# Another written-out order of the pieces, the last output columns in two writes, and w2 in one load

## The chip, the core and the metric

The kernel runs on one NeuronCore of a Trainium2 chip. The metric is the time of one execution on the device in microseconds (us). All engines of the core run side by side, each in its own order: TensorE (PE in the profile, its weight loads PEld), VectorE (DVE), ScalarE (ACT), GpSimd (POOL) and SyncE (SP). SyncE, ScalarE and GpSimd also issue DMAs, which run on 16 DMA engines.

## The reference

A block of 2048 tokens of width 640 (bf16). The input is normalized, and the normalized input feeds two branches whose outputs are added to the input.

```python
def reference(A_x, A_wqkv, A_wo, B_x, B_w1, B_b1, B_w2, B_b2):
    x = A_x                                  # (1, 2048, 640)
    xn = _layernorm(x, axis=-1)
    return x + _A_ref(xn, A_wqkv, A_wo) + _B_ref(xn, B_w1, B_b1, B_w2, B_b2)

# A: 32 heads of 20; each token looks at 8 tokens: itself and those 2, 4, ... 14 before it
qkv    = x @ wqkv
logits = einsum("bhsd,bhswd->bhsw", q, k[gathered]) * 20 ** -0.5   # masked before the start
o      = einsum("bhsw,bhswd->bhsd", softmax(logits), v[gathered])
A      = o @ wo                                                    # 640 x 640
# B: dense, 640 -> 1536 -> 640
B      = gelu_tanh(x @ w1 + b1) @ w2 + b2
```

## The kernel before

The tokens are cut into four chunks of 512 (n = 0 to 3), each into four blocks of 128 (bl). The work is cut into some 700 named pieces. `make_plan` lists them with what they need, and `ORDER` writes out by hand the order in which they are issued. As each engine runs its instructions in the order in which they are issued, `ORDER` sets the order on every engine and every DMA queue at once; when a piece starts is then left to semaphores. A name begins with its kind, and its digits are the chunk and a part:

| pieces | engine | what they do |
|---|---|---|
| `st`, `rs`, `rc`, `xn` | DVE, ACT, DVE, ACT | layernorm: statistics, standard deviation, its reciprocal, normalized x (for chunk 0 DVE normalizes) |
| `tc` | SP | the normalized block transposed by DMA (for chunk 0 `tp` on PE and a copy `tc`) |
| `ga` `gb` `gd` `ge` `gc`, `hj` and `hc` | PE and ACT | projections q, k, v of chunk 0 in parts, and the copies out of PSUM; `hj2..` reads the weights wv |
| `pj`, `pc` | PE, ACT | projections of chunks 1 to 3 (digits: chunk, q/k/v, columns), and the copies out of PSUM |
| `qk`, `lg` | DVE, PE | products q * shifted k for two window places of a pair each; sum over a head's 20 columns into the logits (80 matmuls per chunk) |
| `m` `mx` `ex` `ss` `ri` `at` | DVE (`ex` on ACT) | softmax over the 8 places |
| `xd`, `xs` | SP, ACT | the attention weights written out to all 128 partitions by DMA (tile `ax`), two quarters by each queue |
| `av`, `ad`, `ot` | DVE | products v * weights (8 per chunk), their sums, and oT |
| `f1`, `ge` | PE, ACT | first matmul of the dense branch (12 per chunk) and GELU; hT has 18 buffers |
| `o`, `oc`, `od` | PE, ACT, POOL | output of one block in five parts (four over hT and w2, the fifth over oT and wo), the copy out of PSUM, and the DMA that adds it to the output in DRAM; two buffers osb |
| `xp`, `xb` | SP or ACT, POOL | x copied into the output, and b2 added to it there, by DMA |
| `ld` | SP | the loads of w2, wo and b2 |
| `ohi`, `oclo`, `ochi` | PE, DVE | the last block: its last 128 columns on PE, and the additions of x with the writes to DRAM |

All accumulators of `pj`, `f1`, `hj` and of some `o` share four buffers in PSUM (`acc`). The products of `qk` and `av` share four buffers (`prod`); `prod` of a window pair is free again when its `lg` has read it. For the last block there is no accumulating DMA: `oclo` adds x to the first 512 columns and issues their write from SyncE, then PE does `ohi`, then `ochi` adds x to the last 128 columns and issues their write from ScalarE.

The functions that the change touches, and what calls them, with the lines of the profile:

Of the kernel before, what the change touches and what calls it, by code (L numbers as in the profile page):

```python
# [62 lines left out]
S, D, F, H, W, DIL = 2048, 640, 1536, 32, 8, 2  # L63
P = 128
DH = D // H
PAD = (W - 1) * DIL
KT, FT = D // P, F // P
CH = 512
# [8 lines left out]
LASTB = S // P - 1  # L77
# [5 lines left out]

ORDER = """
pad01 pad02 st00a st00 sm rs00 me nm rc00 sq xn00a xn00b tp00a tp00b tc00a rs01 tb ga tc00b rc01 xn01 gb2 b1 tp01
gb3 tc01a tc01b gb4 gd gc0 ge st03a hj101 gc4 st03 st02a rs03 hj102 st02 hc101 hj100 rs02 hc102 rc02 rc03 gc1 hj200
xn03 xn02 hc100 st11a tp03 tp02 st13a tc03 hj201 st11 tc02 st10a hj202 hc200 st12a hj012 st10 hj010 st13 hc012 hc202
st12 hj111 hc010 hc201 hj011 rs1 hc111 rc1 st21a hj110 hc011 st22a st22 hj112 hc110 st20a hj212 st33a hc112 f102
xn10 qk031 hc212 f100 xn13 tc10 qk001 ge02 f109 qk020 hj210 pad11 tc13 ge09 hj211 qk010 xn11 f108 hc211 qk000 ge00
f101 tc11 qk011 f105 ge01 ge08 qk021 f104 xn12 f1011 tc12 ge04 qk030 f1010 ge011 st23a st21 lg00 ge010 st20 ld lg01  # L90
ge05 st23 lg02 lg03 st31a rs2 pj114 mk m0 pj102 pc114 st32a st30a pj110 pc102 mx0 hc210 pj111 pc110 st32 ex0 pj101
rc2 st31 st30 pj100 st33 pj112 ss0 pc100 pc101 pj104 xn21 ri0 pj103 tc21 pc104 at0 pc111 pj113 pc103 pc112 pj123
pc113 xn23 qk120 f113 pc123 tc23 xn22 f103 qk111 pj121 ge03 qk121 f118 xd0 qk130 ge13 f107 ge18 f112 qk100 ge07
pad21 f106 ge12 qk110 xs0 f115 ge06 qk131 xw0 f110 rs3 qk101 o020 tc22 xn20 o021 ge15 lg10 lg11 av011 lg12 pc121
tc20 lg13 ge10 rc3 pj120 av000 o022 pc120 av031 xn32 o023 pj122 tc32 av021 f111 pc122 m1 xn30 pj124 ge11 av030 tc30
pad12 pj214 av020 pj204 pc214 pj203 pc204 av001 pj211 pc203 av010 pc124 pj202 xn33 mx1 pc211 pj210 tc33 xn31 ad01
pj221 pc210 pc202 pj223 tc31 pj201 ad00 pj220 pc201 pc223 pj213 xp0 pj200 pc213 ad02 pc221 pj212 pc220 pc200 pj224
pc212 ex1 xb0 ot0 pj310 f1110 qk231 pc310 o024 qk220 pj300 oc02 ss1 pad31 od02 o000 o001 qk200 o002 o003 ri1 o004
at1 pj313 qk201 xd1 oc00 o010 pc313 qk211 pc300 pj301 xs1 qk210 o011 o012 qk221 o013 xw1 pj303 qk230 o014 xp1 xb1
lg20 oc01 lg21 av130 pc303 lg22 pc224 lg23 av100 o030 f138 av110 o031 od00 ge38 av111 pj312 o032 pc301 m2 ge110 f117  # L100
pc312 av131 f116 av120 pj304 pj302 mx2 o033 pc302 av121 ge16 f121 ge17 ad11 f1111 xp2 f1210 ge21 xb2 ge111 o034
ge210 av101 pad22 pc304 f119 ad10 pj311 pj222 pc311 xb3 oc03 pj314 ad12 ge19 od01 f114 od03 f125 ge14 pc222 ot1
pj324 pad32 pc314 ex2 o100 qk331 pj322 qk321 o101 ge25 o102 ss2 o103 pj323 ri2 o104 qk330 pc323 pc322 pj320 at2 oc10
pj321 pc320 qk311 xd2 xs2 o110 pc324 qk301 o111 pc321 o112 qk310 f120 qk300 f126 xw2 f130 ge26 qk320 f127 xl lg30
ge27 lg31 av201 lg32 lg33 o113 m3 o114 av211 f1311 oc11 av200 od11 o120 o121 od10 av221 o122 av230 o123 o124 av220
f1211 oc12 mx3 od12 o130 av210 o131 ge20 ge30 f124 ex3 ad20 f123 o132 ge311 o133 av231 o134 ge24 ss3 f128 ge211 oc13
f129 ad21 ge23 f122 ge29 ge28 f131 ge22 ri3 o210 at3 f135 ad22 o211 xd3 f134 f1310 ot2 o212 ge310 ge31 o213 xs3 o214
xw3 f137 oc21 ge34 od21 o220 av311 o221 o222 av300 o223 av310 o224 f136 av321 oc22 od22 o230 av301 o231 od13 o232
av320 o233 av331 o234 av330 f132 oc23 od23 o200 ad31 o201 ge32 ge36 o202 ge37 f139 ad30 f133 ge39 ge35 o203 ge33
o204 ad32 o310 oc20 o311 o300 ot3 o301 o302 o303 o304 o312 oc30 o313 od30 o320 od20 o321 o322 o323 o314 o324 oc31  # L110
od31 o330 oc32 o331 od32 o332 o333 o334 ohi oclo ochi
""".split()


# [173 lines left out]
def kernel(  # L288
# [16 lines left out]
    nc = tc.nc  # L305
# [3 lines left out]
    out_sd = out.rearrange("b s d -> (b s) d")  # L309
# [22 lines left out]
    w2_sb = wts.tile([P, FT, D], BF16, name="w2_sb")  # L332
# [27 lines left out]


    def do_ld():
        w2_v = B_w2.rearrange("(t p) n -> p t n", p=P)
        for c in range(2):
            ts = slice(c * FT // 2, (c + 1) * FT // 2)
            nc.sync.dma_start(w2_sb[:, ts, :], w2_v[:, ts, :])
        nc.sync.dma_start(wo2[:], A_wo.rearrange("(p t) n -> p t n", t=KT))
        nc.sync.dma_start(b2bc[:], b2_bcast)

# [392 lines left out]
    def do_ochi():  # L762
        osb = tiles["osb", last]
        nc.vector.tensor_tensor(  # L764
            out=osb[:, CH:D], in0=tiles["hi", *last][:, 0 : D - CH], in1=x_sb[:, LASTB, CH:D], op=ALU.add
        )
        nc.scalar.dma_start(out_sd[LASTB * P :, CH:D], osb[:, CH:D])

    fns = {k[3:]: v for k, v in locals().items() if k.startswith("do_")}
    engines = {getattr(mybir.EngineType, e) for e in ("PE", "DVE", "Activation", "SP")}  # L770
# [40 lines left out]
```

## Time and profile before

| | |
|---|---|
| median of 13 runs | 212.66 us (212.34 to 216.91) |
| the profiled execution | 212.47 us |
| its span, first to last instruction | 210.5 us |
| granted TensorE clock | 1.00 in every stage |
| busy: PE, DVE, ACT, POOL | 205.5, 173.4, 111.6, 19.8 us |
| matmuls recorded, weight loads recorded | 1511, 1535 |
| bytes moved by DMA | 23.93 MB, 114 GB/s in the mean |

A matmul is recorded with the time until its result is out of the array, 379 ns for 512 columns, while the next one starts 216 ns after it; busy times of an engine are unions, so overlap is not counted twice. "Idle before" is the time for which an engine had stood still when an instruction began, with what ended it; a row with SPq or ACTq is the issue of a DMA, and not the transfer. Some matmul records are missing from a trace.

### The profile page before, as it was taken

To read this page: it belongs to the slowest core of one execution; us is meant where nothing else is said; L and a number is where in the kernel's file an instruction comes from. 1 tells how busy PE (TensorE), PEld (TensorE's weight loads), DVE (VectorE), ACT (ScalarE), POOL (GpSimd) and SP (SyncE) were. 2 spreads that over 40 slices of the span, in tenths; PEclk is the share of its full clock that TensorE was granted. 3 is DMA by queue.
4 is the path that set the end of the run, shared out by engine and by line. 5 is a ranking of instruction groups with operands and counts; after the bars stand their busy time and mean duration, and the time that the engine had idled before them with its cause. 6 is when DMAs were issued, how large, how long until landed. Compare 5 with 4: busy or idle time off the path is not lost.

```text
span 210.5 us, 3645 instructions
## 1 busy us (share of the span) xinstructions
PE 205.5 (98%) x1511; PEld 118.8 (56%) x1535; DVE 173.4 (82%) x178; ACT 111.6 (53%) x193; POOL 19.8 (9%) x37
## 2 busy tenths in 40 slices
PE   8999999999999999999999999999999999999994
PEld 2999656554465555555654555565554455555552
DVE  3487999969979999996899999989999829997001
ACT  6476977889785748330727486321396221441120
POOL 2000000000000002110300600101101011101130
PEclk9999999999999999999999999999999999999999
DMA  6999417914952063559296690721222571212224
GB/s 218 367 364 372 85 36 200 384 42 86 142 68 46 16 189 45 85 91 217 78 156 219 97 152 3 139 93 11 27 28 34 100 125 17 29 27 31 31 27 70
DMA packets 24072, 23.93 MB, mean 114 GB/s; under 512 B 9080, under 2 KB 21880, under 8 KB 24056
## 3 DMA queue, kind: packets, MB, share of 16 engines
q1 hardware_dynamic: 17008, 14.68, 25.6%
q0 software_dynamic: 4144, 4.92, 17.3%
q10 hardware_dynamic: 2904, 4.10, 7.1%
q8 instruction: 12, 0.20, 0.4%
q14 instruction: 4, 0.03, 0.0%
HBM read 10.00 MB, written 7.54 MB: 83 GB/s over the span
## 4 chain that ended last, share of the span: by engine, by line
PE 96%; DMA 1%; issue 1%; ACT 1%; DVE 0%; ACTq 0%
PE lo L734 27%; PE hps L703 24%; PE pps L509 23%; PE hi L736 8%; PE gps L553 6%; PE L L608 4%; PE gps L522 1%; DMA x_sb<-in_A_x_dram 1%; PE tp L465 1%; ACT xn L417 0%; DVE xn L450 0%; ACT std L430 0%; DVE osb L764 0%; DVE rstd L434 0%; ACT L376 0%
## 5 line engine op out<-in xcount | busy, mean ns | idle before, releaser
L703 PE MATMUL hps<-xnT,w_sb 128*128 128x512 bf16 x235 | 55.1, 379 | 0.3
L681 DVE TENSOR_TENSOR pv<-vT,ax 128x2560 bf16<-128x2560 bf16 x32 | 45.8, 1483 | 9.1 <-DMA ax<-attn 7.1
L734 PE MATMUL lo<-w_sb,hT 128*128 128x512 bf16 x184 | 52.9, 379 | 0.1
L583 DVE TENSOR_TENSOR prod<-qT,kT 128x2560 bf16<-128x2560 bf16 x32 | 45.5, 1484 | 1.9 <-ACT kT L568 1.5
L714 ACT ACTIVATE hT<-hps,b1T 128x512 bf16<-128x512 f32 x48 | 31.6, 689 | 18.7 <-PE hps L703 17.2
L736 PE MATMUL hi<-w_sb,hT 128*128 128x128 bf16 x192 | 40.3, 219 | 0.5 <-issue 0.2
L703 PEld LDWEIGHTS <-w_sb 128*128 128x128 bf16 x240 | 22.8, 98 | 26.0
L690 DVE TENSOR_TENSOR pv<-pv 128x5120 bf16<-128x5120 bf16 x12 | 33.7, 2821 | 0.2
L741 ACT CAST osb<-lo 128x512 bf16<-128x512 f32 x15 | 8.8, 586 | 44.7 <-issue 26.7
L734 PEld LDWEIGHTS <-hT 128*128 128x128 bf16 x192 | 18.7, 98 | 22.5 <-issue 0.4
L734 PE MATMUL lo<-wo,oT 128*128 128x512 bf16 x74 | 21.9, 379 | 0.0
L747 POOL DMA_DIRECT2D out_dram<-osb x15 | 13.6, 904 | 86.3 <-ACT osb L742 80.3
L736 PEld LDWEIGHTS <-hT 128*128 128x128 bf16 x192 | 18.4, 98 | 2.7
L509 PE MATMUL pps<-xnT,wk_sb 128*128 128x512 bf16 x73 | 18.2, 379 | 0.1
L509 PE MATMUL pps<-xnT,wv_sb 128*128 128x512 bf16 x72 | 18.0, 379 | 0.1
L509 PE MATMUL pps<-xnT,wq_sb 128*128 128x512 bf16 x75 | 18.0, 379 | 0.1
L736 PE MATMUL hi<-wo,oT 128*128 128x128 bf16 x80 | 16.9, 219 | 0.3
L409 DVE BATCH_NORM_STATS2 stats<-x_sb 128x6 f32<-128x320 bf16 x30 | 13.0, 467 | 4.2 <-DMA x_sb<-in_A_x_dram 4.2
L490 POOL DMA_DIRECT2D out_dram<-b2bc x4 | 5.3, 1466 | 98.4 <-DMA out_dram<-x_sb 98.4
L568 ACT CAST qT<-pps 128x512 bf16<-128x512 f32 x15 | 8.7, 590 | 8.8 <-PE pps L509 8.8
L734 PEld LDWEIGHTS <-oT 128*128 128x128 bf16 x80 | 7.8, 98 | 9.4
L509 PEld LDWEIGHTS <-wk_sb 128*128 128x128 bf16 x75 | 8.6, 118 | 7.2 <-issue 0.2
(75 smaller groups left out, 199.1 us busy)
## 6 DMA issues: line engine op xcount, KB each, us to landing
w_sb<-in_B_w_dram SPq DMA_DIRECT2D x4, 960.0 KB, 11.0
out_dram<-osb POOLq DMA_DIRECT2D x15, 160.0 KB, 3.3
ax<-attn SPq DMA_DIRECT2D x8, 256.0 KB, 4.7
ax<-attn ACTq DMA_DIRECT2D x8, 256.0 KB, 4.3
out_dram<-b2bc POOLq DMA_DIRECT2D x3, 640.0 KB, 6.6
x_sb<-in_A_x_dram SPq DMA_DIRECT2D x1, 1280.0 KB, 13.5
out_dram<-x_sb ACTq DMA_DIRECT2D x1, 1120.0 KB, 4.6
wq_sb<-in_A_wqkv_dram SPq DMA_DIRECT2D x1, 800.0 KB, 4.8
```

Of the source, the lines that this page charges most:

```text
L409: nc.vector.bn_stats(stats[:, i, :], x_sb[:, b, i * (D // 2) : (i + 1) * (D // 2)])
L509: nc.tensor.matmul(ps[:], lhsT=wqkv_p[which][:, ti, to, :], rhs=xnT[:, ti, :], start=(ti == 0), stop=(ti == KT - 1),)
L553: nc.tensor.matmul(ps[:, to - a, :], lhsT=wqkv_p[which][:, ti, to, :], rhs=tiles["xnT", 0][:, ti, pair * 2 * P : (pair + 1) * 2 * P], star ...
L583: nc.vector.tensor_tensor(out=prod[:, i, :, :], in0=qkv_tile(n, 0)[:], in1=qkv_tile(n, 1)[:, :, off : off + CH], op=ALU.mult,)
L681: nc.vector.tensor_tensor(out=pv[:, i, :, :].rearrange("p t (j c) -> p t j c", j=BPC), in0=qkv_tile(n, 2)[:, :, off : off + CH].rearrange( ...
L690: nc.vector.tensor_tensor(out=ta[:], in0=ta[:], in1=tb[:], op=ALU.add)
L703: nc.tensor.matmul(ps[:], lhsT=w1_sb[:, ti, ft * P : (ft + 1) * P], rhs=tiles["xnT", n][:, ti, :], start=(ti == 0), stop=(ti == KT - 1),)
L714: nc.scalar.activation(hT[:], tiles["hps", n, ft][:], ACT.Gelu_apprx_tanh, bias=b1T[:, ft : ft + 1], scale=1.0)
L734: nc.tensor.matmul(lo[:], lhsT=lhs, rhs=rhs[:, 0:CH], start=first, stop=last)
L736: nc.tensor.matmul(hi[:, 0 : D - CH], lhsT=lhs, rhs=rhs[:, CH:D], start=first, stop=last)
L741: nc.scalar.copy(osb[:, 0:CH], tiles["lo", n, bl][:])
L747: nc.gpsimd.dma_start(rows, tiles["osb", n, bl][:], accum_op=ALU.add)
```

## The change

Three edits. `ORDER` is replaced by another order of the same pieces. The last 128 output columns leave by two DMAs of 64 rows each, one issued from SyncE and one from ScalarE, in place of one DMA of 128 rows from ScalarE. And w2 is loaded by one DMA in place of two. The two smaller edits in full:

```diff
     def do_ld():
-        w2_v = B_w2.rearrange("(t p) n -> p t n", p=P)
-        for c in range(2):
-            ts = slice(c * FT // 2, (c + 1) * FT // 2)
-            nc.sync.dma_start(w2_sb[:, ts, :], w2_v[:, ts, :])
+        nc.sync.dma_start(w2_sb[:], B_w2.rearrange("(t p) n -> p t n", p=P))
         nc.sync.dma_start(wo2[:], A_wo.rearrange("(p t) n -> p t n", t=KT))
         nc.sync.dma_start(b2bc[:], b2_bcast)
...
-        nc.scalar.dma_start(out_sd[LASTB * P :, CH:D], osb[:, CH:D])
+        for half, queue in enumerate((nc.sync, nc.scalar)):
+            ps = slice(half * P // 2, (half + 1) * P // 2)
+            rows = slice(LASTB * P + ps.start, LASTB * P + ps.stop)
+            queue.dma_start(out_sd[rows, CH:D], osb[ps, CH:D])
```

Of `ORDER` the first line and a half stay, up to `hj101`; after that nearly every line differs. The places that matter for what follows:

```diff
-gb3 tc01a tc01b gb4 gd gc0 ge st03a hj101 gc4 st03 st02a rs03 hj102 st02 hc101 hj100 rs02 hc102 rc02 rc03 gc1 hj200
-xn03 xn02 hc100 st11a tp03 tp02 st13a tc03 hj201 st11 tc02 st10a hj202 hc200 st12a hj012 st10 hj010 st13 hc012 hc202
+gb3 tc01a tc01b gb4 gd gc0 ge st03a hj101 gc1 st03 st02a rs03 hj100 st02 hc101 gc4 rc03 xn03 hj200 rs02 hc100 rc02
+xn02 tp03 tp02 st10a tc03 hj201 st12a tc02 st11a hj202 st13a hc200 st10 hj010 st12 hj011 st13 hc010 st11 hc201 hj110
...
-pad21 f106 ge12 qk110 xs0 f115 ge06 qk131 xw0 f110 rs3 qk101 o020 tc22 xn20 o021 ge15 lg10 lg11 av011 lg12 pc121
+pc100 f112 pc113 xs0 qk121 f106 xd0 f118 qk120 ge06 f103 qk101 f107 ge03 qk130 pad21 f110 ge07 xw0 xn21 o020 qk100
+ge18 pj121 xn22 qk111 pj123 tc22 qk131 o021 pc123 ge12 f113 qk110 pc121 rs3 f115 tc21 lg10 ge10 rc3 lg11 av020 lg12
...
-pc212 ex1 xb0 ot0 pj310 f1110 qk231 pc310 o024 qk220 pj300 oc02 ss1 pad31 od02 o000 o001 qk200 o002 o003 ri1 o004
-at1 pj313 qk201 xd1 oc00 o010 pc313 qk211 pc300 pj301 xs1 qk210 o011 o012 qk221 o013 xw1 pj303 qk230 o014 xp1 xb1
+pc224 tc30 mx1 o024 pc201 qk221 pj221 oc02 ex1 o000 qk200 o001 qk211 o002 pc221 o003 ss1 o004 ri1 pj303 oc00 at1
+od00 pj310 qk210 xd1 o010 pc310 pj300 qk201 o011 qk230 pj313 o012 pc313 qk231 xs1 o013 o014 qk220 xw1 pj301 xp1 lg20
...
-pj321 pc320 qk311 xd2 xs2 o110 pc324 qk301 o111 pc321 o112 qk310 f120 qk300 f126 xw2 f130 ge26 qk320 f127 xl lg30
+ge27 od10 o110 qk321 pj222 o111 qk320 pc222 pc320 f130 xs2 qk311 f120 pc324 xw2 o112 qk300 f138 lg30 ge38 lg31 av231
...
-f129 ad21 ge23 f122 ge29 ge28 f131 ge22 ri3 o210 at3 f135 ad22 o211 xd3 f134 f1310 ot2 o212 ge310 ge31 o213 xs3 o214
-xw3 f137 oc21 ge34 od21 o220 av311 o221 o222 av300 o223 av310 o224 f136 av321 oc22 od22 o230 av301 o231 od13 o232
+at3 o134 ad20 xd3 f124 oc13 xs3 od13 f123 pad32 od11 f135 ge23 ad22 ge24 f134 ge29 o210 xw3 ge34 o211 ot2 o212 o213
+xl av321 o214 av320 f137 oc21 od21 o220 av301 o221 av331 o222 o223 av311 o224 av310 f136 oc22 od22 o230 av300 o231
...
-o204 ad32 o310 oc20 o311 o300 ot3 o301 o302 o303 o304 o312 oc30 o313 od30 o320 od20 o321 o322 o323 o314 o324 oc31
-od31 o330 oc32 o331 od32 o332 o333 o334 ohi oclo ochi
+o310 ot3 oc20 o311 od20 o300 o301 o302 o303 o304 o312 oc30 o313 od30 o320 o321 o314 o322 oc31 o323 od31 o324 o330
+oc32 o331 od32 o332 o333 o334 ohi oclo ochi
```

More of the change, by code (lines that the diff above doesn't have):

```diff
@@ L85 @@
 pad01 pad02 st00a st00 sm rs00 me nm rc00 sq xn00a xn00b tp00a tp00b tc00a rs01 tb ga tc00b rc01 xn01 gb2 b1 tp01
-gb3 tc01a tc01b gb4 gd gc0 ge st03a hj101 gc4 st03 st02a rs03 hj102 st02 hc101 hj100 rs02 hc102 rc02 rc03 gc1 hj200
-xn03 xn02 hc100 st11a tp03 tp02 st13a tc03 hj201 st11 tc02 st10a hj202 hc200 st12a hj012 st10 hj010 st13 hc012 hc202
-st12 hj111 hc010 hc201 hj011 rs1 hc111 rc1 st21a hj110 hc011 st22a st22 hj112 hc110 st20a hj212 st33a hc112 f102
-xn10 qk031 hc212 f100 xn13 tc10 qk001 ge02 f109 qk020 hj210 pad11 tc13 ge09 hj211 qk010 xn11 f108 hc211 qk000 ge00
@@ L90 @@
[L90 to L93, printed above, removed]
-pad21 f106 ge12 qk110 xs0 f115 ge06 qk131 xw0 f110 rs3 qk101 o020 tc22 xn20 o021 ge15 lg10 lg11 av011 lg12 pc121
@@ L95 @@
-tc20 lg13 ge10 rc3 pj120 av000 o022 pc120 av031 xn32 o023 pj122 tc32 av021 f111 pc122 m1 xn30 pj124 ge11 av030 tc30
-pad12 pj214 av020 pj204 pc214 pj203 pc204 av001 pj211 pc203 av010 pc124 pj202 xn33 mx1 pc211 pj210 tc33 xn31 ad01
-pj221 pc210 pc202 pj223 tc31 pj201 ad00 pj220 pc201 pc223 pj213 xp0 pj200 pc213 ad02 pc221 pj212 pc220 pc200 pj224
-pc212 ex1 xb0 ot0 pj310 f1110 qk231 pc310 o024 qk220 pj300 oc02 ss1 pad31 od02 o000 o001 qk200 o002 o003 ri1 o004
-at1 pj313 qk201 xd1 oc00 o010 pc313 qk211 pc300 pj301 xs1 qk210 o011 o012 qk221 o013 xw1 pj303 qk230 o014 xp1 xb1
@@ L100 @@
[L100 to L103, printed above, removed]
-pj321 pc320 qk311 xd2 xs2 o110 pc324 qk301 o111 pc321 o112 qk310 f120 qk300 f126 xw2 f130 ge26 qk320 f127 xl lg30
@@ L105 @@
-ge27 lg31 av201 lg32 lg33 o113 m3 o114 av211 f1311 oc11 av200 od11 o120 o121 od10 av221 o122 av230 o123 o124 av220
-f1211 oc12 mx3 od12 o130 av210 o131 ge20 ge30 f124 ex3 ad20 f123 o132 ge311 o133 av231 o134 ge24 ss3 f128 ge211 oc13
-f129 ad21 ge23 f122 ge29 ge28 f131 ge22 ri3 o210 at3 f135 ad22 o211 xd3 f134 f1310 ot2 o212 ge310 ge31 o213 xs3 o214
-xw3 f137 oc21 ge34 od21 o220 av311 o221 o222 av300 o223 av310 o224 f136 av321 oc22 od22 o230 av301 o231 od13 o232
-av320 o233 av331 o234 av330 f132 oc23 od23 o200 ad31 o201 ge32 ge36 o202 ge37 f139 ad30 f133 ge39 ge35 o203 ge33
@@ L110 @@
-o204 ad32 o310 oc20 o311 o300 ot3 o301 o302 o303 o304 o312 oc30 o313 od30 o320 od20 o321 o322 o323 o314 o324 oc31
-od31 o330 oc32 o331 od32 o332 o333 o334 ohi oclo ochi
+gb3 tc01a tc01b gb4 gd gc0 ge st03a hj101 gc1 st03 st02a rs03 hj100 st02 hc101 gc4 rc03 xn03 hj200 rs02 hc100 rc02
+xn02 tp03 tp02 st10a tc03 hj201 st12a tc02 st11a hj202 st13a hc200 st10 hj010 st12 hj011 st13 hc010 st11 hc201 hj110
+hc011 st22a st21a hc202 hj111 st22 hc110 st20a hj012 st20 hc111 hj112 rs1 hj102 rc1 hc112 hc012 hj211 hc102 xn10
@@ new lines @@
+qk011 f104 xn13 tc10 qk031 f101 ge04 f108 qk000 ge01 hj210 tc13 ge08 qk020 f1011 hc210 xn11 qk030 f109 ge011 tc11
+hj212 qk010 f1010 hc212 xn12 qk001 f105 ge09 tc12 f100 ge05 qk021 ge010 f102 ge00 st23a st21 lg00 ge02 ld st23 lg01
+st31a lg02 rs2 lg03 pj112 mk st30a hc211 st31 pj101 pad12 pc112 st32a m0 pj102 pc101 pad11 st30 pj103 pc102 mx0
+pj114 pc103 st33a ex0 pj110 st32 rc2 st33 pj111 pc114 pj104 ss0 xn23 pj100 pc110 tc23 ri0 pc111 pj113 pc104 at0
+pc100 f112 pc113 xs0 qk121 f106 xd0 f118 qk120 ge06 f103 qk101 f107 ge03 qk130 pad21 f110 ge07 xw0 xn21 o020 qk100
@@ new lines @@
+ge18 pj121 xn22 qk111 pj123 tc22 qk131 o021 pc123 ge12 f113 qk110 pc121 rs3 f115 tc21 lg10 ge10 rc3 lg11 av020 lg12
+lg13 av021 xn20 pj120 tc20 pj122 av011 o022 pc122 av000 ge15 o023 ge13 f1110 av030 xn33 f111 tc33 av010 pj124 ge11
+av001 pj212 pc124 pj213 av031 pc212 pj223 pc213 ad01 xn31 pj210 pc120 tc31 pj200 pc210 pad22 pj204 ad00 pc200 pj214
+pc204 xp0 pc223 pj220 pc214 ad02 pj203 pc220 xn32 pj202 pc203 xb0 tc32 pj211 pc202 ot0 pj224 pc211 xn30 m1 pj201
+pc224 tc30 mx1 o024 pc201 qk221 pj221 oc02 ex1 o000 qk200 o001 qk211 o002 pc221 o003 ss1 o004 ri1 pj303 oc00 at1
@@ new lines @@
+od00 pj310 qk210 xd1 o010 pc310 pj300 qk201 o011 qk230 pj313 o012 pc313 qk231 xs1 o013 o014 qk220 xw1 pj301 xp1 lg20
+pc301 xb1 lg21 av131 pc300 lg22 oc01 lg23 pad31 av121 f116 o030 av101 pj314 ge16 av120 od01 o031 ge110 o032 av111
+pc314 f117 m2 f1111 ge17 pc303 av110 f125 ge111 o033 ge25 av100 pj304 av130 f114 pc304 xp2 pj311 ad10 xb2 f119 pc311
+pj302 ad11 o034 pc302 pj323 oc03 ge19 pj312 mx2 xb3 ge14 pc323 f1210 ad12 ex2 od02 o100 od03 pj322 pj321 ss2 pc322
+pc312 f126 ge210 ri2 f127 at2 ge26 o101 pc321 qk331 xd2 o102 pj324 ot1 f121 qk310 o103 o104 qk330 pj320 oc10 qk301
@@ new lines @@
+ge27 od10 o110 qk321 pj222 o111 qk320 pc222 pc320 f130 xs2 qk311 f120 pc324 xw2 o112 qk300 f138 lg30 ge38 lg31 av231
+lg32 lg33 av220 o113 o114 m3 f1311 oc11 av210 ge21 o120 mx3 o121 o122 av221 ex3 o123 av230 o124 f1211 ad21 oc12 od12
+o130 o131 ge211 o132 av200 o133 ge20 av211 f128 ge30 f122 ge28 av201 f1310 ss3 f131 ge310 ge311 ri3 f129 ge31 ge22
+at3 o134 ad20 xd3 f124 oc13 xs3 od13 f123 pad32 od11 f135 ge23 ad22 ge24 f134 ge29 o210 xw3 ge34 o211 ot2 o212 o213
+xl av321 o214 av320 f137 oc21 od21 o220 av301 o221 av331 o222 o223 av311 o224 av310 f136 oc22 od22 o230 av300 o231
@@ L112 @@
+av330 o232 o233 ad31 o234 f132 oc23 od23 ad30 o200 o201 ge37 ge32 f133 ge36 ge35 o202 ad32 ge33 o203 f139 o204 ge39
+o310 ot3 oc20 o311 od20 o300 o301 o302 o303 o304 o312 oc30 o313 od30 o320 o321 o314 o322 oc31 o323 od31 o324 o330
+oc32 o331 od32 o332 o333 o334 ohi oclo ochi
 """.split()
```

## Prediction

> **What bounds the kernel now.** I first read the busy line of the page.
>
> ```profile
> PE 205.5 (98%) x1511; PEld 118.8 (56%) x1535; DVE 173.4 (82%) x178; ACT 111.6 (53%) x193; POOL 19.8 (9%) x37
> ```
>
> TensorE is busy nearly all the time, but is it truly back to back? I cut the span between the first useful matmul and the tail into stages (columns: length, then busy time and count of PE, PEld, DVE, ACT, POOL, clock, DMA share, GB/s).
>
> ```profile
> 21.00:60.00 39.00, 38.74 (x294) 21.69 (x301) 34.91 (x46) 33.62 (x50) 0.00 (x0) 1.00 0.55 136
> 60.00:100.00 40.00, 39.74 (x277) 22.18 (x274) 38.14 (x29) 20.32 (x37) 3.19 (x3) 1.00 0.51 95
> 100.00:140.00 40.00, 39.74 (x293) 21.34 (x289) 38.50 (x28) 21.95 (x38) 6.57 (x6) 1.00 0.59 123
> 140.00:180.00 40.00, 39.63 (x313) 21.68 (x307) 34.63 (x25) 15.08 (x26) 4.29 (x5) 1.00 0.32 48
> ```
>
> PE lacks 0.26 to 0.37 us in each. The page line says why: 1511 matmuls stand against 1535 weight loads, so 24 matmul records are missing, and each leaves an apparent hole of some 0.05 us. PE is therefore gapless from 5.3 us to 207.8 us at full clock. No matmul is added or removed, so a new order can't shorten this stretch by more than the 0.3 us that I can't account for. It can only open holes in it. What is left to win is the tail, which I read last.
>
> ```profile
> 206.63 0.83 PE L736 MATMUL hi<-w_sb,hT 128*128 128x128 bf16 x12
> 206.89 0.69 DVE L755 TENSOR_TENSOR osb<-lo,x_sb 128x512 bf16<-128x512 f32 x1 [13.33 <-PE lo L734]
> ...
> 207.61 0.36 SPq L756 DMA_DIRECT2D out_dram<-osb  x1
> 207.78 0.29 DVE L764 TENSOR_TENSOR osb<-hi,x_sb 128x128 bf16<-128x128 f32 x1 [0.20 <-PE hi L736]
> 208.11 0.35 ACTq L767 DMA_DIRECT2D out_dram<-osb  x1
> ```
>
> ```profile
> out_dram<-osb SPq DMA_DIRECT2D x1, 128.0 KB, 1.7
> out_dram<-osb ACTq DMA_DIRECT2D x1, 32.0 KB, 1.5
> ```
>
> The last write is issued at 208.11 and lands 1.5 us later, at 209.6; 0.9 us of closing steps end the span at 210.5. The profiled execution took 212.47 us, 1.97 more than its span. The median of the 13 runs is 212.66.
>
> **The tail, part by part.** Four times the bytes (128 KB against 32 KB) land only 0.24 us later, so 1.4 us of the last write is fixed. Halving 32 KB is worth 16/96 of 0.24, or 0.04 us. SyncE is free for its half: its earlier issue ends at 207.97, before the last addition ends at 208.07. I take -0.05 us. Bounds: -0.35, if an issue costs nothing any more, and +0.36, if the second issue stands behind the first. The Trainium skill speaks against this edit: "DMA: Bandwidth & Descriptors", section "Rules for kernel authors", says of two transfers to disjoint partition halves not to bother, because both halves spread over the same 16 engines and serialize; by it the sum gets 0 here. No row of this profile has such a pair.
>
> **w2 in one load.** It removes one SyncE issue of 0.58 us. The halves landed at 37.8 and 41.8 us; one load lands whole by about 41.8. What changes is that the first output group o020 must wait for all of it. That group moves ahead of four groups (f113, f115, pj121, pj123, 4 x 1.08 = 4.3 us), from 57.1 to 52.8 us. The cover is still 11 us of other matmuls. Cost 0; without cover it would be what the load is late.
>
> **The order.** I checked each place where a piece moved closer to what it needs, by adding durations ahead of it. Three matter.
>
> *First value matmul, hj200.* The old order put hj102 (5 matmuls of 0.109 = 0.54 us) before it; the new one puts that later.
>
> ```profile
> 9.43 2.89 PE L553 MATMUL gps<-xnT,wk_sb 128*128 128x256 bf16 x25
> 12.16 1.25 PE L553 MATMUL gps<-xnT,wv_sb 128*128 128x256 bf16 x10
> ```
>
> The weights wv are issued at 2.80 and take 8.9 us, so they land at 11.7. PE's weight load started at 12.1; now it could at 11.56. It waits some 0.15 plus the wake-up: +0.2 us. Bounds 0 (an earlier landing) and 0.54 (all of the piece). Everything queued behind it on PE shifts, and nothing later gives this back.
>
> *Logits of chunk 3, lg30.* This is the place I fear most. The expansion of the attention weights (ax) of chunk 1 is issued half by SyncE and half by ScalarE (xs1). On ScalarE's queue xs1 stands behind the copy pc313, which waits for the matmuls pj313. The new order puts pj303, o010 and o011 ahead of pj313: 1.08 + 2 x 0.82 = 2.7 us. Now the rows of before, ScalarE's and then VectorE's:
>
> ```profile
> 92.96 0.59 ACT L568 CAST kT<-pps 128x512 bf16<-128x512 f32 x1 [0.38 <-PE pps L509]
> 93.12 0.55 ACTq L665 DMA_DIRECT2D ax<-attn  x1
> 93.44 0.59 ACT L568 CAST qT<-pps 128x512 bf16<-128x512 f32 x1
> 93.70 1.65 ACTq L665 DMA_DIRECT2D ax<-attn  x1
> ```
>
> ```profile
> 100.92 5.70 DVE L681 TENSOR_TENSOR pv<-vT,ax 128x2560 bf16<-128x2560 bf16 x4 [2.58 <-DMA ax<-attn]
> 139.25 0.48 DVE L493 TENSOR_TENSOR x_sb<-x_sb,b2bc 128x640 bf16<-128x640 bf16 x1
> 172.21 11.30 DVE L681 TENSOR_TENSOR pv<-vT,ax 128x2560 bf16<-128x2560 bf16 x8 [4.54 <-DMA ax<-attn]
> ```
>
> xs1 moves from 93.12 to 95.8, with the 0.2 above to 96.0. In before it took 7.8 us until VectorE could start (100.92), since all four pieces and two other writes shared the DMA engines, which were 92% to 100% busy from 94 to 100 us. For chunk 3, ScalarE's pair was issued alone at 167.29, and VectorE started 4.9 us later (172.21). In the new order SyncE's pair has had 4 us by then, so I take the row of the lone pair: 96.0 + 4.9 = 100.9, as before. Between this start and the last product of chunk 3 VectorE does the same 25 pieces in both orders, 139.25 - 100.92 = 38.3 us without idle time. They end at 139.25 again, and lg30 starts on PE at 139.65, now 139.85. In before the last product was qk320, which only the third logits piece (139.65 + 1.0) reads; now it is qk300, which lg30 itself reads, so 1 us of cover is gone and 0.5 is left. I take +0.1 us for it; bounds 0 and, at 7.8 us instead of 4.9, 2.9 - 0.5 = 2.4.
>
> *Accumulators.* PE has four PSUM accumulators, and at f113, pj200 and f130 it now takes one whose copy ends within about 0.1 us of the moment it is needed. In before pj301 stood equally close: its copy ended at 92.96 + 0.59 = 93.55, its first matmul began at 93.59, and no hole is seen. I take +0.1 us in all, bounds 0 and 0.6 (three copies each 0.2 late).
>
> *The other moved steps* keep their cover. xs0 goes from 54.4 to about 47.4 us and its reader still starts at 59.9. On SyncE's queue xp0 now stands ahead of two transposes of chunk 3 instead of behind them; the last of them goes out near 82.1, lands 2.6 us later, and is read at 89.5. On GpSimd's queue od02 goes out behind xb2 and xb3 near 121 us instead of at 87.8, so one of the two output buffers is held that long and oc01, oc03 and oc10 take turns on the other or wait for its write: od00 goes out near 90.7 and lands within the 6.6 us that a crowded write took in before, at 97.3, for oc01 at 102. ScalarE loads its tables as often as before. Cost 0 each; without cover, what the transfer is late.
>
> *What gets better without gain here.* The last output projection o304 began at 194.00 in before, and the oT that it reads was finished only at 193.56. In the new order the third softmax comes one addition (2.8 us) earlier, and xs3 no longer waits behind GELUs fed at 167 us. VectorE's last block can start about 3.4 us earlier than 172.21. In this execution the cover of 0.4 us held, so nothing is gained; in a run where the DMA was late it would be. The 13 runs reach up to 216.91 and their median lies 0.19 above the profiled one. I take -0.1 us on the median for fewer such runs. Next late is then lg30.
>
> **Sum.** -0.05 + 0 + 0.2 + 0.1 + 0.1 = +0.35 us: 212.47 becomes 212.8 in a profiled execution. On the median 212.66 + 0.35 - 0.1 = 212.9 us.
>
> **The rivals.**
>
> *Slower: ax of chunk 1 lands late.* The deciding point is VectorE's start on that block at 101.4 us; each microsecond later opens a hole of one microsecond before lg30. Against it: the queue is emptier when xs1 goes out. For it: od00 and the 640 KB copy xp1 still share the 16 engines, and in before the same pair took 7.8 us. At that figure 212.8 + 2.4 = 215.2; half of it gives 214.0.
>
> *Faster: the late runs vanish and nothing stalls.* wv comes in time, every copy makes it, the tail gives 0.35: 212.47 - 0.35 = 212.1. A gain of over 1.06 us would need shorter PE work, and the stages above show no hole to close.
>
> *The edit doesn't do what it says.* The halves of the last write may land no earlier than one write, and o020 could stand waiting for the whole w2. The first changes 0.05 us; the second needs a load 11 us late. Time 212.9 to 213.2.
>
> **Numbers.** Forecast 0.60, faster rival 0.19, slower rival 0.16, no-effect rival 0.05. What a measurement of this kernel can tell from no change is about 0.5%, 1.06 us: 211.6 to 213.7. The forecast, the no-effect rival and nearly all of the faster one fall inside; 0.13 of the slower rival falls outside, and 0.05 of the forecast, where its upper bounds (0.54 + 0.6 + 0.36) meet. 0.03 of the faster rival stays for holes that the missing records hide. Faster 0.03, same 0.79, slower 0.18. The range goes from 212.2, just above the faster rival's end, to 214.2, which takes in half of the slower one.
>
> **What would show it.** Right: a PE hole of about 0.2 us before the first wv matmul near 11.6 us; xs1 issued near 96; VectorE's second ax block starting near 101; no wait before the logits near 139.9; the last ax block starting near 169; the last matmul near 208.2. Wrong: PE idle for more than 0.5 us in any stage, above all just before 140 us, or PE ending before 207.8.

## The result, and the profile after

The changed kernel takes 214.3 us in the median of 11 runs (213.99 to 217.06), the kernel before 212.59 us in 48. The medians differ by 1.7 us, 0.8%. The ratio of the means, which take in longer executions, is 1.0104, with a 95% interval of 1.0077 to 1.0132: slower by about 1%. The forecast was 212.9 us and no difference, with a range that ended at 214.2 and 0.5% as what can be told from no change, so it was wrong in the size and in the verdict. Some executions of either kernel are 2 to 5 us longer than the rest; the three of the changed kernel show a mean granted TensorE clock of 0.992, its other nine 0.998 to 1.000.

The profiled execution took 214.25 us with a span of 212.3, against 212.47 and 210.5: 1.8 us to be found. First the page's busy line and the stages, as for the kernel before.

```profile
PE 205.7 (97%) x1511; PEld 118.2 (56%) x1535; DVE 173.5 (82%) x178; ACT 111.7 (53%) x193; POOL 19.8 (9%) x37
```

```profile
21.00:60.00 39.00, 38.28 (x267) 21.08 (x273) 34.59 (x44) 31.13 (x49) 0.00 (x0) 1.00 0.50 137
60.00:100.00 40.00, 39.74 (x284) 22.44 (x280) 38.58 (x29) 22.59 (x37) 3.19 (x3) 1.00 0.45 85
100.00:140.00 40.00, 39.74 (x282) 21.27 (x286) 37.68 (x27) 21.01 (x35) 6.59 (x6) 1.00 0.66 133
140.00:180.00 40.00, 39.32 (x311) 21.33 (x315) 37.50 (x29) 16.26 (x28) 4.29 (x5) 1.00 0.28 46
```

PE does the same work. The middle stages are as full as before (39.74), and that includes the place before 140 us that I feared. The first stage has lost 38.74 - 38.28 = 0.46 us, the last 39.63 - 39.32 = 0.31. PE's time line shows where, one hole in each (in brackets the idle time before the row, and what ended it).

```profile
48.78 2.32 PE L700 MATMUL hps<-xnT,w_sb 128*128 128x512 bf16 x10
51.56 1.67 PE L700 MATMUL hps<-xnT,w_sb 128*128 128x512 bf16 x7 [0.46 <-ACT hT L711]
...
162.68 2.32 PE L700 MATMUL hps<-xnT,w_sb 128*128 128x512 bf16 x10
165.32 1.24 PE L700 MATMUL hps<-xnT,w_sb 128*128 128x512 bf16 x5 [0.31 <-ACT hT L711]
```

The groups that wait are f110 and f134, and both wait for a GELU (line 711) that frees their accumulator. The rows count from the end of the last matmul, which takes 0.379 us to come out, whereas the next could have begun 0.216 after its start; so each hole costs 0.16 us more than its bracket, 0.62 and 0.48 us. What did ScalarE do just before?

```profile
46.83 0.58 ACT L565 CAST kT<-pps 128x512 bf16<-128x512 f32 x1 [0.32 <-PE pps L506]
47.06 2.44 ACTq L662 DMA_DIRECT2D ax<-attn  x2
49.53 1.28 ACT L711 ACT_TABLE_LOAD   x1 [2.12 <-issue]
50.83 1.27 ACT L711 ACTIVATE hT<-hps,b1T 128x512 bf16<-128x512 f32 x2
...
162.05 0.57 ACTq L662 DMA_DIRECT2D ax<-attn  x1
162.27 0.27 ACT L739 CAST osb<-hi 128x128 bf16<-128x128 f32 x1
162.66 1.73 ACTq L662 DMA_DIRECT2D ax<-attn  x1
164.43 0.25 ACT L572 COPY vT<-vT 128x70 bf16<-128x70 bf16 x1 [1.88 <-issue]
164.58 1.84 ACT L711 ACTIVATE hT<-hps,b1T 128x512 bf16<-128x512 f32 x3
```

Its queue is in the issue of its half of the expansion, xs0 and xs3. The second of the two DMAs holds it for 1.73 us, the engine stands still for 2.12 and 1.88 us, and only then come the GELUs (for xs0 behind a table load). SyncE issues its own half, xd0 and xd3, at nearly the same moments:

```profile
47.05 1.30 SPq L662 DMA_DIRECT2D ax<-attn  x2
161.25 1.19 SPq L662 DMA_DIRECT2D ax<-attn  x2
```

The first matmul on wv waits too, and that is the small hole I had forecast.

```profile
9.32 2.35 PE L550 MATMUL gps<-xnT,wk_sb 128*128 128x256 bf16 x20
11.64 1.29 PE L550 MATMUL gps<-xnT,wv_sb 128*128 128x256 bf16 x10
```

From the start of the group before to the first matmul on wv, 25 matmuls took 12.16 - 9.43 = 2.73 us in the kernel before. Now 20 take 11.64 - 9.32 = 2.32, where 20 x 0.109 = 2.18 would do: 0.14 us lost. Only 0.06 remain at the first projection of chunk 1, because the pieces ahead of this place had run a little sooner in this execution. The tail:

```profile
208.76 0.36 SPq L753 DMA_DIRECT2D out_dram<-osb  x1
208.94 0.29 DVE L761 TENSOR_TENSOR osb<-hi,x_sb 128x128 bf16<-128x128 f32 x1 [0.20 <-PE hi L733]
209.25 0.55 SPq L767 DMA_DIRECT2D out_dram<-osb  x1
209.26 0.58 ACTq L767 DMA_DIRECT2D out_dram<-osb  x1
```

```profile
out_dram<-osb SPq DMA_DIRECT2D x1, 128.0 KB, 1.7
out_dram<-osb SPq DMA_DIRECT2D x1, 16.0 KB, 1.8
out_dram<-osb ACTq DMA_DIRECT2D x1, 16.0 KB, 2.0
```

The last addition starts at 208.94 instead of 207.78, 1.16 us later: 0.62 + 0.48 + 0.06. Each half of the last write is issued in 0.55 to 0.58 us, where the whole took 0.35, and lands 1.8 and 2.0 us after its issue instead of 1.5: +0.55. Some 0.07 lie in the closing steps. Together 1.78, the whole difference of the spans.

### The profile page after: what moved, and what is told of

Read it like the earlier page. It is cut to its first block, busy times and chain, and to the rows that moved or that the text cites. A ratio compares the mean times of both kernels' runs of the same rounds, so it can differ in the third digit from the quotient of the medians.

```text
span 212.3 us, 3636 instructions
## 1 busy us (share of the span) xinstructions
PE 205.7 (97%) x1511; PEld 118.2 (56%) x1535; DVE 173.5 (82%) x178; ACT 111.7 (53%) x193; POOL 19.8 (9%) x37
## 4 chain that ended last, share of the span: by engine, by line
PE 90%; DMA 2%; ACTq 2%; ACT 2%; issue 1%; SPq 0%; DVE 0%
PE lo L731 26%; PE pps L506 23%; PE hps L700 21%; PE hi L733 8%; PE gps L550 7%; PE L L605 4%; DMA wq_sb<-in_A_wqkv_dram 2%; ACTq L662 2%; PE gps L519 1%; ACT hT L711 1%; ACT L711 1%; PE tp L462 0%; ACT kT L565 0%; SPq L342 0%; DVE osb L761 0%
## 5 line engine op out<-in xcount | busy, mean ns | idle before, releaser
L711 ACT ACTIVATE hT<-hps,b1T 128x512 bf16<-128x512 f32 x48 | 30.9, 686 | 14.4 <-PE hps L700 13.1
L731 PE MATMUL lo<-wo,oT 128*128 128x512 bf16 x77 | 22.5, 379 | 0.1
L744 POOL DMA_DIRECT2D out_dram<-osb x15 | 14.3, 957 | 86.6 <-ACT osb L739 86.6
L506 PE MATMUL pps<-xnT,wq_sb 128*128 128x512 bf16 x72 | 17.5, 379 | 0.1
L752 DVE TENSOR_TENSOR osb<-lo,x_sb 128x512 bf16<-128x512 f32 x1 | 0.7, 692 | 16.1 <-PE lo L731 16.1
L565 ACT CAST kT<-pps 128x512 bf16<-128x512 f32 x15 | 8.7, 587 | 9.1 <-PE pps L506 9.1
```

Of the source, the lines that this page charges most:

```text
L506: nc.tensor.matmul(ps[:], lhsT=wqkv_p[which][:, ti, to, :], rhs=xnT[:, ti, :], start=(ti == 0), stop=(ti == KT - 1),)
L565: nc.scalar.copy(dest[:, to, off : off + CH], tiles["pps", n, which, to][:])
L711: nc.scalar.activation(hT[:], tiles["hps", n, ft][:], ACT.Gelu_apprx_tanh, bias=b1T[:, ft : ft + 1], scale=1.0)
L731: nc.tensor.matmul(lo[:], lhsT=lhs, rhs=rhs[:, 0:CH], start=first, stop=last)
L744: nc.gpsimd.dma_start(rows, tiles["osb", n, bl][:], accum_op=ALU.add)
```

## The experiments

**One last write again, in the changed kernel.**

```diff
-        for half, queue in enumerate((nc.sync, nc.scalar)):
-            ps = slice(half * P // 2, (half + 1) * P // 2)
-            rows = slice(LASTB * P + ps.start, LASTB * P + ps.stop)
-            queue.dma_start(out_sd[rows, CH:D], osb[ps, CH:D])
+        nc.scalar.dma_start(out_sd[LASTB * P :, CH:D], osb[:, CH:D])
```

> The changed kernel with the last 128 columns in one write of 128 rows from ScalarE again. Theory (the split itself costs: the two issues at once took 0.55 and 0.58 us against 0.35, and the later half landed 2.05 us after its issue against 1.50): 0.55 to 0.6 us faster than the changed kernel, about 213.7 us, last landing 1.5 us after its issue. Rival (the late landing comes with the new order, whose od31 and od32 writes stand closer to the end, and not with the split): no faster, 214.2 us, and a last landing near 2 us.

213.85 us; 1.0059 of the kernel before (1.0046 to 1.0072), and 0.45 less than the changed kernel in the median. The two holes of PE stay (first row: us waited in all, times, longest), the last write lands 1.5 us after its issue:

```profile
PE hps L700 <- ACT hT L711: 0.7, 2, 0.4
```

```profile
209.09 0.35 ACTq L764 DMA_DIRECT2D out_dram<-osb  x1
```

The late landing belongs to the split.

**The split alone, in the kernel before** (the same edit the other way round).

> The kernel before with only the split of the last write. Theory (the split itself costs): 0.5 to 0.6 us slower than the kernel before, about 213.0 us, issues near 0.55 us each, PE without a hole as before. Rival (the late landing comes with the new order): within 0.1 us of the kernel before.

213.38 us against 212.53; 1.0042 (1.0028 to 1.0056), or 0.6 to 1.2 us. PE has no hole. The time line and the DMA rows of this kernel repeat what the changed one showed:

```profile
207.88 0.56 SPq L770 DMA_DIRECT2D out_dram<-osb  x1
207.88 0.59 ACTq L770 DMA_DIRECT2D out_dram<-osb  x1
```

```profile
out_dram<-osb ACTq DMA_DIRECT2D x1, 16.0 KB, 2.1
```

The two runs agree: the split costs, in either order of the pieces.

**Both halves from ScalarE, in the changed kernel.** Is it the two queues at the same moment, or the 64 rows?

```diff
-        for half, queue in enumerate((nc.sync, nc.scalar)):
+        for half, queue in enumerate((nc.scalar, nc.scalar)):
```

> The changed kernel with both halves of the last write issued from ScalarE, one behind the other. Theory A (issuing at the same moment from two queues slows both issues): 0.35 us each, so the second goes out 0.35 us after the first and lands about 1.85 us after the first issue; 0.1 to 0.2 us faster than the changed kernel. Theory B (a write of 64 rows costs 0.55 us of issue by itself): 1.1 us of issue, last landing about 2.5 us after the first issue, 0.4 us slower than the changed kernel.

214.58 us (1.0099, 1.0082 to 1.0117). The issues, from this kernel's time line:

```profile
209.22 1.21 ACTq L767 DMA_DIRECT2D out_dram<-osb  x2
```

They take 0.56 and 0.62 us, although no other queue issues beside them. That is theory B: the half write is dear by itself. The second one lands 2.45 us after the first issue.

**Halves by columns, in the kernel before.** Two writes at the same moment, each of 128 rows x 64 columns.

```diff
-        nc.scalar.dma_start(out_sd[LASTB * P :, CH:D], osb[:, CH:D])
+        for c, queue in enumerate((nc.sync, nc.scalar)):
+            cs = slice(CH + c * (D - CH) // 2, CH + (c + 1) * (D - CH) // 2)
+            queue.dma_start(out_sd[LASTB * P :, cs], osb[:, cs])
```

> The kernel before with the last write split by columns: two writes of 128 rows x 64 columns, from SyncE and ScalarE. Theory (it is the 64 rows that cost: 0.56 us of issue each even one behind the other on one queue): issues of 0.35 us, last landing 1.5 us after, the time of the kernel before within 0.1 us. Rival (any two writes at the same moment slow each other): issues of 0.55 us and 0.5 to 0.9 us slower, as with the split by rows.

```profile
210.84 0.34 SPq L769 DMA_DIRECT2D out_dram<-osb  x1
210.85 0.37 ACTq L769 DMA_DIRECT2D out_dram<-osb  x1
```

```profile
out_dram<-osb SPq DMA_DIRECT2D x1, 16.0 KB, 1.4
out_dram<-osb ACTq DMA_DIRECT2D x1, 16.0 KB, 1.6
```

Same bytes, same two queues, and the issues are back at 0.35 us. So 0.2 us of each issue belong to the form of the write (64 rows) and not to the company; the landings are 1.4 and 1.6 us. The halves by rows landed 0.4 us later than these, counted from the issue: 0.2 of it is the longer issue, the rest comes behind it and is not explained. The time, 212.97 against 212.58 us (1.0028, 0.9987 to 1.0069), doesn't tell a small loss from none; the 0.1 us of the theory was not met in the median. It is no gain.

**xs0 and xs3 later, in the changed kernel.**

```diff
-pc100 f112 pc113 xs0 qk121 f106 xd0 f118 qk120 ge06 f103 qk101 f107 ge03 qk130 pad21 f110 ge07 xw0 xn21 o020 qk100
-ge18 pj121 xn22
+pc100 f112 pc113 qk121 f106 xd0 f118 qk120 ge06 f103 qk101 f107 ge03 qk130 pad21 f110 ge07 xn21 o020 qk100
+ge18 xs0 xw0 pj121 xn22
...
-at3 o134 ad20 xd3 f124 oc13 xs3 od13 f123 pad32 od11 f135 ge23 ad22 ge24 f134 ge29 o210 xw3
+at3 o134 ad20 xd3 f124 oc13 od13 f123 pad32 od11 f135 ge23 ad22 ge24 f134 ge29 xs3 o210 xw3
```

> The changed kernel with ScalarE's half of two expansions issued later: xs0 from behind pc113 to behind ge18, xs3 from behind oc13 to behind ge29, so that the GELUs for f110 and f134 stand ahead of them on ScalarE. Theory (ScalarE stands 2.4 us in these issues, the GELUs behind them free their accumulators late, and PE waits 0.62 us before f110 and 0.48 us before f134): both holes close, 1.1 us faster than the changed kernel, about 213.2 us. Rival (the holes come from the accumulators being taken too closely whatever ScalarE does): the holes stay within 0.2 us of their size, 214.0 us or more.

213.25 us in the median, 1.05 less than the changed kernel (measured apart from it); 1.0040 of the kernel before (1.0010 to 1.0071), with the split tail still in it. The stages and the issues of this kernel:

```profile
21.00:60.00 39.00, 39.00 (x295) 21.67 (x297) 34.77 (x45) 31.83 (x50) 0.00 (x0) 1.00 0.54 137
140.00:180.00 40.00, 40.00 (x318) 21.71 (x311) 37.94 (x28) 16.04 (x28) 4.29 (x5) 1.00 0.29 48
```

```profile
L662 ACTq DMA_DIRECT2D ax<-attn x8: 551/613/647, 52.2 to 164.1; - x8
```

Both holes are gone, and (the three numbers after x8 are ns: least, median, most) no issue of an expansion on ScalarE takes over 0.65 us now. In the changed kernel the longest is 1732 ns. Two things changed at once here, though: the place of xs0 and the length of its issue.

**Only xd0 later, first try.** To keep xs0 in its place and take SyncE's pair away, xd0 went from behind f106 to behind ge07.

```diff
-f106 xd0 f118
+f106 f118
...
-f110 ge07 xw0
+f110 ge07 xd0 xw0
```

> The changed kernel with xs0 where it is and SyncE's half xd0 issued later, from behind f106 to behind ge07. Theory (ScalarE's second issue took 1.73 us only because SyncE's queue issued its two at the same time, 47.05 and 47.77 us): ScalarE's pair goes out in 0.6 + 0.6 us, its table load starts near 48.4 instead of 49.5 us, the hole before f110 closes, and the kernel is about 0.6 us faster than the changed one, 213.7 us; the hole before f134 stays. Rival (this pair takes ScalarE 2.4 us in any case): the hole stays at 0.6 us, 214.2 us.

214.01 us (1.0081, 1.0058 to 1.0104), and the hole is as large as before. But nothing of SyncE's queue stands between the two places, so the pair still goes out with ScalarE's:

```profile
47.62 2.43 ACTq L662 DMA_DIRECT2D ax<-attn  x2
```

```profile
47.62 1.30 SPq L662 DMA_DIRECT2D ax<-attn  x2
```

The edit moved a name and no instruction. It tells nothing of the theory.

**Only xd0 later, behind the transpose tc22.**

```diff
-f106 xd0 f118
+f106 f118
...
-f110 ge07 xw0
+f110 ge07
...
-pj123 tc22 qk131
+pj123 tc22 xd0 xw0 qk131
```

> The changed kernel with xs0 where it is and SyncE's half xd0 behind the transpose tc22, which waits for ScalarE until about 55.7 us. Theory (ScalarE's second issue took 1.73 us only because SyncE's pair went out at the same time): ScalarE's pair takes 0.6 + 0.6 us near 47 us, its table load starts near 48.4 us and the hole before f110 closes. The expansion then lands near 62 us, so VectorE starts its block late by some 2 us, and the total may be worse; only the hole near 51 us is to be judged. Rival: ScalarE's second issue takes 1.7 us again and the hole stays at 0.6 us.

A single execution, 215.28 us, worse as expected: VectorE is late, and PE waits near 83 us. SyncE's, ScalarE's and then PE's time line at the place in question:

```profile
56.67 1.30 SPq L662 DMA_DIRECT2D ax<-attn  x2
```

```profile
47.31 1.30 ACTq L662 DMA_DIRECT2D ax<-attn  x2
48.63 1.28 ACT L711 ACT_TABLE_LOAD   x1 [0.98 <-issue]
```

```profile
47.73 5.56 PE L700 MATMUL hps<-xnT,w_sb 128*128 128x512 bf16 x25
```

xs0 stands where it stood, takes 0.65 + 0.61 us, and the 25 matmuls run without a hole. So the second issue took 1.73 us because of SyncE's pair beside it, and that extra 1.1 us made the hole before f110. The pair need not go out at the same moment: in the kernel before, SyncE's pair was 1.75 us ahead (91.37 us), and ScalarE's second issue, at 93.70, took 1.65 us. The run with xs0 and xs3 later moved xs3 to 2.9 us behind SyncE's pair, where its second issue took 0.62 us, and behind the GELUs at once; which of the two closed the hole before f134 was not separated.

**w2 in two loads in the changed kernel; w2 in one load in the kernel before.** The edit of the change's first part, once taken back and once made alone.

> The changed kernel with w2 in two loads again. Theory (the load is hidden behind 11 us of matmuls either way): within 0.1 us of the changed kernel, 214.2 to 214.4 us. Rival (the one load of 1.9 MB delays the loads behind it and the transposes): 0.2 us or more faster.

> The kernel before with only w2 in one load. Theory (hidden either way): within 0.2 us of the kernel before. Rival (the longer load pushes back wo, b2 and the transposes behind it): 0.2 us or more slower.

214.62 us, 1.0100 (1.0079 to 1.0121), the same as the changed kernel's 1.0104; and 212.65 against 212.41 us, 1.0024 (0.9990 to 1.0058). No effect is to be seen. The interval of the latter reaches up to 1.2 us, but in its profile, of 213.07 us, w2 is loaded from 33 us on, and PE is busy for 39.00, 40.00, 40.00 and 40.00 us in the four stages from 21 to 180 us. What makes this execution longer than 212.47 lies ahead of the load.

**All taken back but the rest of the order.** xs0 and xs3 later, one last write, and in the head:

```diff
-hj100 st02 hc101 gc4 rc03 xn03 hj200 rs02 hc100 rc02
+hj100 st02 hc101 gc4 hj102 rc03 xn03 hj200 rs02 hc100 hc102 rc02
...
-rs1 hj102 rc1
+rs1 rc1
...
-hj211 hc102 xn10
+hj211 xn10
```

once with w2 in one load and once in two.

> The changed kernel with the three costs taken back: xs0 and xs3 issued later, one last write, and hj102 with its copy hc102 ahead of hj200 again; w2 in one load stays. Theory: PE without a hole, tail as before, so the time of the kernel before within 0.2 us, 212.3 to 212.7 us. Rival (the new order brings more accumulator waits than the two holes): over 213.0 us. A gain on the kernel before by over 0.3 us would say that PE has work to lose that I don't see.

> The changed kernel with xs0 and xs3 later, one last write, hj102 ahead of hj200, and w2 in two loads: all that is left of the change is the rest of the new order. Theory (the order's costs are the two holes alone): the kernel before within 0.2 us, 212.3 to 212.6 us. Rival (the one load of w2 was the 0.1 to 0.2 us by which the version with it stayed above the kernel before): then this one is that much faster than it; without that, it stays 0.2 us above the kernel before.

212.95 us against 212.41 (1.0044, 1.0019 to 1.0070), and 212.98 against 212.58 (1.0035, 0.9994 to 1.0076). The profiled execution of the second has the span of the kernel before, 210.5 us, and 212.50 us in all. The stages of its profile have no hole:

```profile
21.00:60.00 39.00, 38.97 (x297) 21.45 (x299) 34.79 (x47) 31.94 (x50) 0.00 (x0) 1.00 0.53 137
140.00:180.00 40.00, 40.00 (x318) 21.68 (x307) 37.21 (x28) 16.02 (x28) 4.30 (x5) 1.00 0.29 48
```

So in the profiled execution the change owes its whole loss to the places named. Of these, hj102 was not taken back alone. The medians lie above the kernel before all the same, by 0.5 us in the first and 0.2 to 0.4 in the second (without and with its two longest executions), and the execution profiled of the second is the shortest of its twelve. The interval of the first excludes equality, that of the second does not; where such a rest would come from, if it is there, stays open. No version here beats the kernel before.

## Why the prediction was wrong, point by point

*No hole to close.* Right. PE was gapless, and the best version's profile only reaches the old span again.

*xs0.* This is the step that failed. The prediction said that xs0 goes from 54.4 to about 47.4 us, that its reader still starts at 59.9, and "Cost 0". It asked who reads the data and not who stands behind the issue on ScalarE's queue: a table load and the GELUs ge06, ge03 and ge07, the first of which frees the accumulator that f110 needs at once. And moving xs0 forward put it at the same moment as xd0. The time line of before had the price: at 132.35 us, the one place where both pairs went out together, ScalarE's two issues took 2.47 us against 1.2 to 1.3 where they went out alone. Its rows, ScalarE's and then SyncE's:

```profile
54.38 1.29 ACTq L665 DMA_DIRECT2D ax<-attn  x2
132.35 2.47 ACTq L665 DMA_DIRECT2D ax<-attn  x2
```

```profile
132.35 1.21 SPq L665 DMA_DIRECT2D ax<-attn  x2
```

Even the prediction's own rows show it: the issue at 93.70 took 1.65 us. With this price the sum would have had a term of up to about 1 us for xs0 where it stands, and one for xs3 (an estimate from the 1.2 us by which the pair took longer; how much of it PE feels depends on the cover). In place of 0 the runs showed 0.62 us for xs0.

*xs3.* The prediction entered it as a relief, since it "no longer waits behind GELUs". The GELUs now wait behind it. Its pair again met SyncE's (161.25 and 162.05 us), and PE lost 0.48 us.

*The tail.* -0.05 was taken, with bounds of -0.35 and +0.36; it measured +0.55 in the profile and 0.6 to 1.2 in the kernel before with the split alone. This is the second step that failed, a term of the wrong size. It came from a line through two writes of 128 rows each, 128 KB and 32 KB. That line knows nothing of rows, and half of the rows at the same row length is not what it describes. The rule of the Trainium skill that was set against the edit ("DMA: Bandwidth & Descriptors", "Rules for kernel authors": don't bother with two transfers to disjoint partition halves, use one of 128 partitions) pointed the right way. These runs agree with its advice, and show a loss where it speaks of the halves sharing the same engines: 0.35 us of issue became 0.56, even with both halves on one queue.

*hj200.* Right in kind: +0.2 was taken, 0.14 us of hole is seen and 0.06 is left later.

*lg30.* Right, though it came close. xs1 went out at 96.50 (forecast 96.0, and PE was 0.7 late by then) and VectorE began the block at 102.19, just 0.1 past the deciding point of 101.4 once it is moved by the same 0.7.

```profile
102.19 1.49 DVE L678 TENSOR_TENSOR pv<-vT,ax 128x2560 bf16<-128x2560 bf16 x1 [3.00 <-PE L L605]
```

PE shows no new hole before 140 us. Of the two rows to choose from, the lone pair's 4.9 us was the nearer one: from issue to VectorE's start it took 5.7. The data were there after 5.5, and the profile puts the end of VectorE's wait down to the logits on PE.

*Accumulators, w2, the other moved steps.* f113, pj200 and f130 show no hole above 0.02 us; 0.1 was taken. w2 costs nothing that these profiles show.

*The -0.1 on the median.* Wrong. VectorE's last block did move ahead (170.05 us, although PE was 1.2 us later than before), but the long executions did not get rarer (over 1.5 us above the lowest: 7 of 48 before, 3 of 11 after). Two profiles of long executions are there, one of the first version with all taken back (214.93 us) and one of the halves by columns (215.56 us), and both lose their time at the start. The first matmul on wk comes at 11.38 and 12.17 us, where the other version with all taken back and the kernel before have it at 9.23 and 9.43: 2.15 and 2.74 of the 2.4 and 3.1 us by which their spans are longer.

```profile
9.23 2.89 PE L553 MATMUL gps<-xnT,wk_sb 128*128 128x256 bf16 x25
11.38 2.78 PE L550 MATMUL gps<-xnT,wk_sb 128*128 128x256 bf16 x24
12.17 2.02 PE L553 MATMUL gps<-xnT,wk_sb 128*128 128x256 bf16 x17
```

The stage ahead of it, of the two long ones:

```profile
5.50:10.00 4.50, 4.06 (x39) 3.63 (x39) 1.62 (x7) 1.62 (x6) 0.00 (x0) 0.65 1.06 369
5.50:10.00 4.50, 2.83 (x27) 2.57 (x27) 0.96 (x5) 0.73 (x3) 0.00 (x0) 0.71 1.06 370
```

PE waits there for the load of wq (0.29 and 1.40 us), and its granted clock is 0.65 and 0.71 against 1.00 in the kernel before. The pieces up to this point stand in the same order in both kernels, and the first expansion goes out after 47 us, so late expansions are not what made these two long. What delays the start was not tried, and the three long executions of the changed kernel itself were not profiled.

The slower rival was given 0.16 for one named mechanism, the third logits. The loss came by another: an issue that blocks the queue of an engine that feeds PE. The sign was on the list, the place was not.

## What to carry to other kernels

When a DMA issue is moved, cost it on the engine that issues it: write down what stands behind it in that queue, and how long the issue took in the profile where another queue issued beside it, and only then ask whether the data comes in time. Where the bounding engine runs without gaps, every engine that frees its buffers has a due time, and 1 us of blocked queue is enough to open a hole though that engine is half idle. A small last write is here nearly all fixed cost (1.4 of 1.5 us, estimated from two writes); splitting it gained nothing by columns and lost by rows.

## What the runs showed of the hardware

- An expansion is issued as two DMAs of 256 KB from SyncE and two from ScalarE, four times per execution, and 13 profiled executions are on record. In 20 of these 52 cases SyncE's pair went out 0 to 1.75 us ahead of ScalarE's, and ScalarE's second issue took 1.56 to 2.18 us, once 0.88. In 31 it went out 2.9 us or more ahead, in one 9.4 us behind, and ScalarE's second issue took 0.61 to 0.63. Nothing lies between 1.75 and 2.9 us. ScalarE's first issue took 0.55 to 0.69 us in every case, SyncE's issues 0.54 to 0.68, but for one of 1.24. Why it is ScalarE's second one was not tried.
- A write of 64 rows x 128 columns (16 KB) took 0.55 to 0.62 us to issue, one of 128 rows x 128 columns (32 KB) 0.35, one of 128 rows x 64 columns (16 KB) 0.34 to 0.37. Of the two 16 KB writes the one with fewer rows took longer to issue. Why was not tried.
